# Channels grouped by five neighbours instead of by stride: input chunks turned before the first transform

## The chip, the cores and the metric

The kernel runs on one core of a Trainium2 chip. The core has five engines with queues of their own: TensorE (PE in the profile; its weight loads are listed apart as PEld), VectorE (DVE), ScalarE (ACT), GpSimd (POOL) and SyncE (SP, which only issues DMAs here). The metric is the device time of one execution in microseconds; three runs gave 457.33, 458.6 and 460.24, so the median is 458.6 us.

## The reference, cut to what matters

Eight sequences of 3200 positions with 256 channels go through a filter in the frequency domain and then through a gated linear unit whose gate is a short causal convolution:

```
X = rfft(x, axis=1);  Y = X * (filt_r + 1j*filt_i)
y = irfft(Y, n=3200, axis=1)
gate_pre[:, t] = sum over k of conv_w[k] * y[:, t-4+k]        # 5 taps, zeros in front
gate = 1 / (1 + exp(-gate_pre))
out  = (gate * (y @ w_val)) @ w_out
```

x and out are float32 of shape (8, 3200, 256), the filters (1601, 256), w_val and w_out (256, 256), conv_w (5, 256).

## The kernel before, in words

A sequence of 3200 is split as 128 x 25 (L = 128, R = 25): a transform of length 128, then one of length 25. The input of one batch lies in SBUF as a tile xb[128, 25, 260] in bf16: 25 rows of channels per partition, where 256 channels are padded to 260 = 52 x 5 (ND = 52, J = 5). The transform of length 25 is done for 5 channels at once, on 125 = 25 x 5 partitions (P2). Which five channels share a group is what the change is about: before, group g has the channels g, g + 52, g + 104, g + 156 and g + 208, so in the flattened free dimension of xb its 125 elements (25 rows, 5 channels) are one run with a step of 52. Eight chunks of 6 or 7 groups in turn (CH, line 24) cover the 52 groups of a batch.

One step G of the main loop (lines 470 to 492) handles one chunk in each stage of a software pipeline; a batch is eight steps, and there are 64 chunks:

- load_x (line 87): the rows of x for later batches, as GpSimd DMAs that cast float32 to bf16, two DMAs for nearly every row, 49 per batch. They are emitted some 25/8 rows per step, one batch ahead, into three buffers xb. The loads of batch 0 stand in the prologue.
- s1 (lines 315 to 325): for each group one matmul. The group's 125 strided elements are the stationary operand (lhsT), the cosine and sine table cf_t[128, 128] the moving one; the result is evicted by VectorE to sob.
- s2 (lines 327 to 354): four matmuls for the length 25, an eviction by ScalarE to xsb, and three products on VectorE (za, zb, z) with the filter tables fr_t and fm_t.
- inva (lines 356 to 373): the first half of the inverse, four matmuls per group in two column halves of 64, evicted by ScalarE to u[128, 25, 260].
- invb (lines 375 to 397): the second half, matmuls with a slice of u as stationary operand, evicted by ScalarE to yt; for the first piece of a batch, GpSimd copies four rows of yt for the convolution's history.
- conv (lines 399 to 414): the five taps as matmuls on 64 x 64 quarters of the array, sigmoid on ScalarE.
- val and outp (lines 416 to 452): the two dense layers, the gate product on VectorE between them, the output's eviction by VectorE (even pieces) or ScalarE (odd ones), and its DMA on SP.

The order within a step is written out by hand: load_x, invb, s1, conv, s2, val, inva, outp. A stage works on an older chunk the further back it stands: s2 one step behind s1, inva three, invb eleven (a batch must be complete), conv thirteen, val fourteen and outp fifteen. The framework gives each engine a queue in about this order and inserts the semaphores. All stages take their PSUM tile from one pool of four tiles (two banks each), in the order of the stages: a tile can be written once the eviction of the stage four tiles back is done.

Before the loop, a prologue makes the tables. For each of the two filters, GpSimd DMAs bring 13 + 12 rows in bf16 (lines 141 and 146), matmuls with a reversal matrix rev turn the order of 12 of them (line 233), an eviction puts them into gf (lines 239, 241), 52 matmuls with strided stationary operands turn the groups onto partitions (line 249), and further matmuls with a selection matrix ex (line 270) bring them into the order of the tables; ScalarE and VectorE evict.

Of the kernel before, what the change touches and what calls it, by code (L numbers as in the profile page):

```python
# [17 lines left out]
R = 25  # L18
J = 5
P2 = R * J  # L20
ND = 52
W = 66
UW = ND * J
# [8 lines left out]
def kernel(  # L32
# [47 lines left out]
    def load_x(b, r):  # L80
        xt = xb[b % NX]
        na = min(L, -(-(S - L * r) // R))
        for a0, a1, s in ((0, na, L * r), (na, L, L * r + R * na - S)):
            if a1 > a0:
                src = bass.AP(tensor=x.tensor, offset=x.offset + (b * S + s) * D,
                              ap=[[R * D, a1 - a0], [1, D]])
                nc.gpsimd.dma_start(out=xt[a0:a1, r, 0:D], in_=src)  # L87

    C2, S2, SN2 = (tb_t[0:P2, i].rearrange("p k j -> p (k j)") for i in (0, 1, 2))

    with tc.tile_pool(name="gen", bufs=1) as g1, tc.tile_pool(name="gen2", bufs=2) as g2:
# [45 lines left out]
        gf, gh = [], []  # L137
        for i, f in enumerate((filt_r, filt_i)):
            g = g1.tile([65, R, UW], BF16, name=f"gf{i}")
            nc.vector.memset(g[:, :, D:UW], 0.0)  # L140
# [4 lines left out]
            h = g1.tile([65, 12, D], BF16, name=f"gh{i}")  # L145
            nc.gpsimd.dma_start(
                out=h[...],
                in_=bass.AP(tensor=f.tensor, offset=f.offset + 64 * D,
                            ap=[[D, 65], [L * D, 12], [1, D]]))
            gh.append(h)  # L150
            gf.append(g)
        for t in xb:
            nc.vector.memset(t[:, :, D:UW], 0.0)
# [5 lines left out]
        for r in range(R):  # L159
            load_x(0, r)  # L160
# [55 lines left out]
        rev = g1.tile([128, 65], BF16, name="rev")  # L216
        nc.vector.tensor_scalar(rev[...], kt65[...], q64[:, 0:1], None, op0=ALU.is_equal)

        ps = psum()
# [5 lines left out]

        nc.vector.memset(fr_t[:, :, 65:W], 0.0)
        nc.vector.memset(fm_t[:, :, :, 65:W], 0.0)
        for i, g in enumerate(gf):
            gv = g[...].rearrange("p m d -> p (m d)")
            for h in range(3):  # L230
                ps = psum()
                for s in range(2):
                    nc.tensor.matmul(ps[0:65, 512 * s:512 * s + 512], lhsT=rev[0:65, :],
                                     rhs=gh[i][:, 4 * h + 2 * s:4 * h + 2 * s + 2, :],
                                     start=True, stop=True)
                dst = g[:, 13 + 4 * h:17 + 4 * h, 0:D]
                pv = ps[0:65, :].rearrange("p (m d) -> p m d", m=4)
                if i == 0:
                    nc.scalar.activation(dst, pv, AF.Copy)
                else:  # L240
                    nc.vector.tensor_copy(dst, pv)
            t1 = g1.tile([128, ND, 65], BF16, name=f"ft{i}")
            for h in range(4):
                ps = psum()
                for s, (o, n) in enumerate(((0, 6), (6, 7))):
                    for a in range(n):
                        d0 = 13 * h + o + a
                        lhs = gv[:, d0:d0 + (P2 - 1) * ND + 1:ND]
                        nc.tensor.matmul(ps[0:P2, 512 * s + 65 * a:512 * s + 65 * a + 65],
                                         lhsT=lhs, rhs=idb[0:65, 0:65],  # L250
                                         start=True, stop=True)
                for s, (o, n) in enumerate(((0, 6), (6, 7))):
                    dst = t1[0:P2, 13 * h + o:13 * h + o + n, :].rearrange(
                        "p g k -> p (g k)")
                    pv = ps[0:P2, 512 * s:512 * s + 65 * n]
                    if i == 0:
                        nc.scalar.activation(dst, pv, AF.Copy)
                    else:
                        nc.vector.tensor_scalar(dst, pv, sg[0:P2, 0:1], None, op0=ALU.mult)
            units = [(0, 3, 3), (3, 3, 3), (6, 3, 3), (9, 3, 3), (12, 3, 3),  # L260
                     (15, 4, 2), (19, 4, 2), (23, 2, 2)]
            for v in range(0, 8, 2):
                ps = psum()
                for s in range(2):
                    u0, nu, nt = units[v + s]
                    n = ND * nt
                    for uu in range(nu):
                        u = u0 + uu
                        w0 = (R - u) * J
                        nc.tensor.matmul(  # L270
                            ps[0:P2, 512 * s + n * uu:512 * s + n * (uu + 1)],
                            lhsT=exf[0:P2, w0:w0 + P2],
                            rhs=t1[0:P2, :, u:u + R * (nt - 1) + 1:R],
                            start=True, stop=True)
                    pv = ps[0:P2, 512 * s:512 * s + n * nu].rearrange(
                        "p (u g t) -> p g t u", u=nu, g=ND)
# [12 lines left out]
        cw = g1.tile([128, 2, K], FP32, name="cw")  # L289
        for dh in range(2):  # L290
# [1 line left out]
                out=cw[:, dh, :],  # L292
                in_=moe_conv_w[:, 128 * dh:128 * dh + 128].rearrange("k d -> d k"))
            for r in range(2):
                ch = 128 * dh + 64 * r
                nc.gpsimd.dma_start(  # L296
                    out=wv_t[:, dh, :].rearrange("p (r h j) -> p h r j", r=2, h=2)[:, r],
                    in_=moe_w_val[128 * dh:128 * dh + 128, 128 * r:128 * r + 128]
                    .rearrange("p (h j) -> p h j", h=2))
                nc.gpsimd.dma_start(out=wo_t[64 * dh:64 * dh + 64, r, :],  # L300
                                    in_=moe_w_out[ch:ch + 64, :])
# [10 lines left out]
    opool = ctx.enter_context(tc.tile_pool(name="ost", bufs=3))  # L312

    st = {}
    def s1(b, c):
        g0, nd = CH[c]
        xf = xb[b % NX][...].rearrange("p r d -> p (r d)")
        ps = psum()
        for i in range(nd):
            lhs = xf[:, g0 + i:g0 + i + (P2 - 1) * ND + 1:ND]  # L320
            nc.tensor.matmul(ps[0:P2, 128 * i:128 * i + 128], lhsT=lhs, rhs=cf_t[:, :],  # L321
                             start=True, stop=True)
        so = sob[(NF * b + c) % 4]
        nc.vector.tensor_copy(so[0:P2, 0:nd, 1:SW - 1],  # L324
# [30 lines left out]

    def inva(b, c):
        if c == 0:
            st[("U", b)] = upool.tile([128, R, UW], BF16, name="u")
        u = st[("U", b)]
        g0, nd = CH[c]  # L360
        z = st.pop(("Z", b, c))
# [1 line left out]
        for i in range(nd):  # L363
            o = 128 * i
            for lo, blk, s0, tab, first in ((0, 0, 1, C2, True), (64, 1, 0, C2, True),
# [1 line left out]
                nc.tensor.matmul(ps[lo:lo + 64, o:o + P2],  # L367
                                 lhsT=z[0:P2, blk, i, s0:s0 + 64], rhs=tab,
                                 start=first, stop=not first)
        nc.scalar.activation(  # L370
            u[:, :, :].rearrange("p r (j g) -> p r j g", j=J)[:, :, :, g0:g0 + nd],
            ps[:, :].rearrange("p (g m) -> p g m", m=128)[:, 0:nd, 0:P2]
            .rearrange("p g (r j) -> p r j g", j=J), AF.Copy)

    def invb(b, j):
        if j == 0:
# [77 lines left out]


    NS = NF * B
    for b in (0, 1):
        pass
    queue = [(b, r) for b in range(1, B) for r in range(R)]
    done = 0  # L460

# [6 lines left out]
    LAG_IA = 3  # L468
    LAG_IB = LAG_IA + NF
    for G in range(NS + LAG_IB + 8):  # L470
        want = min(len(queue), (G + 8) * R // NF)
        while done < want:
            load_x(*queue[done])
            done += 1
        c = back(G, LAG_IB)
        if c is not None:
            invb(*c)
        if G < NS:
            s1(*divmod(G, NF))
        c = back(G, LAG_IB + 2)  # L480
        if c is not None:
            conv(*c)
        if 0 <= G - 1 < NS:
            s2(*divmod(G - 1, NF))
        c = back(G, LAG_IB + 3)
        if c is not None:
            val(*c)
        if 0 <= G - LAG_IA < NS:
            inva(*divmod(G - LAG_IA, NF))
        c = back(G, LAG_IB + 4)  # L490
        if c is not None:
            outp(*c)


# [28 lines left out]
```

## Time and profile before

| | |
|---|---|
| median of three runs | 458.6 us (457.33 to 460.24) |
| the profiled execution | 458.49 us, of which the profile's span is 456.8 us |
| granted TensorE clock, mean | 0.998 |
| busy: PE / PEld / DVE / ACT / POOL | 421.6 / 316.5 / 296.0 / 255.4 / 222.5 us |
| S1 matmuls (line 321), 416 of them | 101.6 us busy, their weight loads 96.6 us |
| DMA issues of x on POOL (line 87), 392 of them | 201.8 us busy, 573 ns each |
| evictions: line 324 / 338 / 370 / 390 / 411 | 65.6 / 56.2 / 67.0 / 52.1 / 52.2 us |

How to read the lines that follow: a group line has the source line, the engine, the operation, output and input tiles, their shapes and the number of instructions; then busy time in us and the mean of one in ns; then the idle time of the engine just before these instructions, with what ended it. A timeline line has the start and the length in us, engine, line, operation and number of instructions merged into it. Listed lengths of matmuls and weight loads overlap each other, so the pace of a run of them is read from start to start. A line of the waits has the total in us, the number and the longest.

### The profile page before, as it was taken

The numbers are of one execution on the slowest core, as the hardware profiler recorded it, in microseconds if no ns is written. First come the engines' busy times: TensorE is split into PE (matmuls) and PEld (weight loads), VectorE is DVE, ScalarE is ACT, GpSimd is POOL, SyncE is SP. The second block draws the span as 40 slices with busy tenths as digits, with TensorE's granted clock in tenths as the row PEclk, the third lists the DMA queues.
The fourth block names the chain that finished last, engine by engine and source line by source line (L and its number), as shares of the span: only waits on it lengthen the run. The fifth ranks groups of instructions, "written<-read, shape, count | busy, mean of one in ns | idle before, by whom it ended". The sixth has DMA issues, their size and how long they took to land.

```text
span 456.8 us, 10880 instructions
## 1 busy us (share of the span) xinstructions
PE 421.6 (92%) x4616; PEld 316.5 (69%) x4647; DVE 296.0 (65%) x465; ACT 255.4 (56%) x287; POOL 222.5 (49%) x440
## 2 busy tenths in 40 slices
PE   0797879988999999999999999999999999999994
PEld 0585868876776767777777777777777776766562
DVE  8116368875766766676767677657776766766364
ACT  1320144566666666666566656566666566657852
POOL 7499999899997439901991089500010001000100
PEclk9999999999999999999999999999999999999999
DMA  8966656465587438711782158421212022113324
GB/s 100 88 64 60 67 63 69 52 68 59 63 159 139 93 68 156 143 70 56 132 157 70 72 99 156 101 82 47 93 66 86 7 89 82 71 47 127 145 115 193
DMA packets 49713, 41.99 MB, mean 92 GB/s; under 512 B 13390, under 2 KB 42496, under 8 KB 49664
## 3 DMA queue, kind: packets, MB, share of 16 engines
q0 software_dynamic: 40288, 15.07, 30.9%
q1 hardware_dynamic: 9376, 26.22, 14.5%
q8 instruction: 36, 0.59, 0.5%
q14 instruction: 13, 0.11, 0.1%
HBM read 30.07 MB, written 26.21 MB: 123 GB/s over the span
## 4 chain that ended last, share of the span: by engine, by line
PE 72%; POOL 20%; DMA 3%; ACT 2%; issue 1%; DVE 1%; DVEq 0%; POOLq 0%
POOL xb L87 18%; PE ps L321 16%; PE ps L406 13%; PE ps L367 10%; PE ps L440 9%; PE ps L423 9%; PE ps L388 5%; PE ps L333 4%; DMA gh<-in_filt_i_dram 3%; PE ps L335 2%; PE ps L334 2%; PE ps L336 2%; ACT u L370 2%; POOL wv_t L296 1%; POOL wo_t L300 0%
## 5 line engine op out<-in xcount | busy, mean ns | idle before, releaser
L87 POOL DMA_DIRECT2D xb<-in_x_dram x392 | 201.8, 573 | 59.6 <-PE ps L321 43.3
L428 DVE TENSOR_TENSOR gv<-ps,gt 128x1024 bf16<-128x1024 f32 (+1 forms) x56 | 62.2, 1111 | 72.9 <-PE ps L423 69.5
L321 PE MATMUL ps<-cf_t,xb 128*125 128x128 f16 x416 | 101.6, 385 | 0.0
L321 PEld LDWEIGHTS <-xb 128*125 128x125 bf16 x416 | 96.6, 312 | 1.2 <-issue 0.2
L411 ACT ACTIVATE gt<-ps 128x1024 bf16<-128x1024 f32 (+1 forms) x56 | 52.2, 933 | 70.5 <-PE ps L406 63.4
L324 DVE CAST sob<-ps 125x768 bf16<-125x768 f32 x64 | 65.6, 1025 | 31.8 <-PE ps L321 31.4
L370 ACT ACTIVATE u<-ps 128x750 bf16<-128x750 f32 x64 | 67.0, 1047 | 31.8 <-PE ps L367 31.7
L338 ACT ACTIVATE xsb<-ps 125x780 bf16<-125x780 f32 x64 | 56.2, 878 | 27.2 <-PE ps L336 24.2
L406 PE MATMUL ps<-yt,dg_t 64*64 64x512 bf16 (+1 forms) x1120 | 65.3, 358 | 1.4 <-POOL yt L397 1.4
L397 POOL COPY yt<-yt 128x508 bf16<-128x508 bf16 x16 | 9.7, 643 | 113.1 <-ACT yt L390 113.1
L367 PEld LDWEIGHTS <-z 125*64 125x64 bf16 x1664 | 48.7, 110 | 23.1 <-issue 22.4
L367 PE MATMUL ps<-tb_t,z 125*64 125x125 f16 x1664 | 59.1, 220 | 0.0
L390 ACT ACTIVATE yt<-ps 128x1024 bf16<-128x1024 f32 (+1 forms) x56 | 52.1, 930 | 12.1 <-PE ps L388 11.3
L440 PE MATMUL ps<-wo_t,gv 128*128 128x256 bf16 x400 | 53.3, 274 | 0.9 <-DVE gv L428 0.9
L423 PE MATMUL ps<-yt,wv_t 128*128 128x512 bf16 (+1 forms) x193 | 50.8, 352 | 1.7
L349 DVE TENSOR_TENSOR za<-xsb,fr_t 125x792 bf16<-125x792 bf16 x64 | 38.7, 604 | 15.0 <-ACT xsb L338 15.0
L440 PEld LDWEIGHTS <-gv 128*128 128x128 bf16 x400 | 35.2, 98 | 10.7 <-DVE gv L428 1.2
L406 PEld LDWEIGHTS <-dg_t 64*64 64x64 bf16 x1120 | 28.0, 106 | 18.9 <-issue 2.3
L352 DVE TENSOR_TENSOR z<-za,zb 125x792 bf16<-125x792 bf16 x64 | 39.1, 611 | 0.8
L445 DVE COPY o<-ps 128x1024 f32<-128x1024 f32 (+1 forms) x32 | 36.8, 1151 | 3.9 <-PE ps L440 3.9
L351 DVE TENSOR_TENSOR zb<-xsb,fm_t 125x792 bf16<-125x792 bf16 x64 | 38.8, 607 | 0.0
L388 PE MATMUL ps<-ci_t,u 128*128 128x128 f16 x400 | 31.8, 219 | 4.1 <-ACT u L370 4.1
(93 smaller groups left out, 341.2 us busy)
## 6 DMA issues: line engine op xcount, KB each, us to landing
out_dram<-o SPq DMA_DIRECT2D x32, 512.0 KB, 2.9
out_dram<-o SPq DMA_DIRECT2D x24, 384.0 KB, 2.3
xb<-in_x_dram POOLq DMA_DIRECT2D x8, 64.0 KB, 2.4
xb<-in_x_dram POOLq DMA_DIRECT2D x8, 61.5 KB, 2.6
xb<-in_x_dram POOLq DMA_DIRECT2D x8, 61.0 KB, 2.5
xb<-in_x_dram POOLq DMA_DIRECT2D x8, 59.0 KB, 2.4
xb<-in_x_dram POOLq DMA_DIRECT2D x8, 58.5 KB, 2.9
xb<-in_x_dram POOLq DMA_DIRECT2D x8, 56.5 KB, 2.5
```

The costliest lines, as they stand in the source:

```text
L87: nc.gpsimd.dma_start(out=xt[a0:a1, r, 0:D], in_=src)
L321: nc.tensor.matmul(ps[0:P2, 128 * i:128 * i + 128], lhsT=lhs, rhs=cf_t[:, :], start=True, stop=True)
L324: nc.vector.tensor_copy(so[0:P2, 0:nd, 1:SW - 1], ps[0:P2, 0:nd * 128].rearrange("p (g k) -> p g k", g=nd))
L338: nc.scalar.activation(xs[0:P2, :, 0:nd, 0:65], ps[0:P2, :].rearrange("p (c n) -> p c n", c=2)[:, :, 0:65 * nd] .rearrange("p c (g k) -> p ...
L367: nc.tensor.matmul(ps[lo:lo + 64, o:o + P2], lhsT=z[0:P2, blk, i, s0:s0 + 64], rhs=tab, start=first, stop=not first)
L370: nc.scalar.activation(u[:, :, :].rearrange("p r (j g) -> p r j g", j=J)[:, :, :, g0:g0 + nd], ps[:, :].rearrange("p (g m) -> p g m", m=12 ...
L388: nc.tensor.matmul(ps[:, o:o + L], lhsT=u[:, r, 128 * dh:128 * dh + 128], rhs=cw_[:, sh:sh + L], start=True, stop=True)
L406: nc.tensor.matmul(ps[64 * dh:64 * dh + 64, 512 * r:512 * r + np_ * L], lhsT=dg_t[rows, dh, k, :], rhs=y[rows, dh, p0 + k:p0 + k + np_, :] ...
L411: nc.scalar.activation(g[:, :, 0:np_ * L], ps[:, :].rearrange("p (h n) -> p h n", h=2)[:, :, 0:np_ * L], AF.Sigmoid)
L423: nc.tensor.matmul(ps[:, 512 * eh:512 * eh + np_ * L], lhsT=wv_t[:, dh, 128 * eh:128 * eh + 128], rhs=y[:, dh, H + p0:H + p0 + np_, :], st ...
L428: nc.vector.tensor_tensor(gv[:, :, 0:np_ * L], ps[:, :].rearrange("p (h n) -> p h n", h=2)[:, :, 0:np_ * L], g[:, :, 0:np_ * L], op=ALU.mult)
L440: nc.tensor.matmul(ps[:, D * a:D * a + D], lhsT=gv[:, eh, L * a:L * a + L], rhs=wo_t[:, eh, :], start=(eh == 0), stop=(eh == 1))
```

## The change

A group now holds five neighbouring channels: group g has the channels 5g to 5g + 4. The last group would reach over the end, so it takes the channels 251 to 255 (a helper, split, gives it apart), and the padding to 260 goes away. For S1's stationary operand, each chunk of x is first copied ("turned") from xb, where a group's five channels are a run in each of 25 rows, into a small tile xpb where the 125 elements of a group lie side by side. ScalarE does this for the even chunks and for all chunks of batch 0, GpSimd for the odd chunks of the other batches, two steps ahead of S1; there are four tiles xpb. The eviction of inva writes runs of whole groups; for the last chunk it is two instructions.

In the prologue, the filter rows come in float32 by SP DMAs instead of GpSimd DMAs with a cast; ScalarE (real part) and VectorE (imaginary part) turn them into the same grouped layout, each time in two instructions because of the last group; the reversal matmuls are in float32 now. The tile t1 has its two free dimensions exchanged, so that the next matmuls read runs of 52. The loads of x for batch 0 stand ahead of some memsets. The DMAs of w_val and w_out move from the prologue into step 0, behind the loads of batch 1.

In the loop, the order within a step becomes load_x, invb, s1, s2, val, outp, conv, inva, with the turn of the chunk two steps ahead in front: conv and inva, which use parts of the array, now follow each other.

```
-    xb = [cpool.tile([128, R, UW], BF16, name=f"xb{i}") for i in range(NX)]
+    xb = [cpool.tile([128, R, D], BF16, name=f"xb{i}") for i in range(NX)]
+    NP = 4
+    xpb = [cpool.tile([128, 7, P2], BF16, name=f"xpb{i}") for i in range(NP)]
...
+    def split(g0, nd):
+        if g0 + nd < ND:
+            return [(0, nd, J * g0)]
+        return [(0, nd - 1, J * g0), (nd - 1, nd, D - J)]
+
+    def permute(b, c):
+        g0, nd = CH[c]
+        xt = xb[b % NX]
+        xp = xpb[(NF * b + c) % NP]
+        for i0, i1, d0 in split(g0, nd):
+            dst = xp[:, i0:i1, :].rearrange("p g (r j) -> p g r j", j=J)
+            src = xt[:, :, d0:d0 + J * (i1 - i0)].rearrange("p r (g j) -> p g r j", j=J)
+            if c % 2 and b > 0:
+                nc.gpsimd.tensor_copy(dst, src)
+            else:
+                nc.scalar.activation(dst, src, AF.Copy)
...
-            g = g1.tile([65, R, UW], BF16, name=f"gf{i}")
-            nc.gpsimd.dma_start(
-                out=g[:, 0:13, 0:D],
+            g = g1.tile([65, 13, D], FP32, name=f"gd{i}")
+            nc.sync.dma_start(
+                out=g[...],
...
+            def turn(m0, nm, src):
+                for i0, i1, d0 in split(0, ND):
+                    ev(q[:, i0:i1, m0:m0 + nm, :],
+                       src[:, :, d0:d0 + J * (i1 - i0)].rearrange(
+                           "p m (g j) -> p g m j", j=J))
+            turn(0, 13, gd[i])
             for h in range(3):
                 ps = psum()
...
-                        lhs = gv[:, d0:d0 + (P2 - 1) * ND + 1:ND]
+                                         lhsT=qv[:, 13 * h + o + a, :],
...
 def s1(b, c):
-            lhs = xf[:, g0 + i:g0 + i + (P2 - 1) * ND + 1:ND]
-            nc.tensor.matmul(ps[0:P2, 128 * i:128 * i + 128], lhsT=lhs, rhs=cf_t[:, :],
+            nc.tensor.matmul(ps[0:P2, 128 * i:128 * i + 128], lhsT=xp[:, i, :], rhs=cf_t[:, :],
...
 def inva(b, c):
+        pv = ps[:, :].rearrange("p (g m) -> p g m", m=128)[:, :, 0:P2]
+        for i0, i1, d0 in split(g0, nd):
+            nc.scalar.activation(
+                u[:, :, d0:d0 + J * (i1 - i0)].rearrange("p r (g j) -> p r g j", j=J),
+                pv[:, i0:i1, :].rearrange("p g (r j) -> p r g j", j=J), AF.Copy)
...
     for G in range(NS + LAG_IB + 8):
+        if G == 0:
+            permute(0, 0)
+            permute(0, 1)
+        if G + 2 < NS:
+            permute(*divmod(G + 2, NF))
...
+        if G == 0:
+            load_w()
         c = back(G, LAG_IB)
         if c is not None:
             invb(*c)
         if G < NS:
             s1(*divmod(G, NF))
-        c = back(G, LAG_IB + 2)
-        if c is not None:
-            conv(*c)
         if 0 <= G - 1 < NS:
             s2(*divmod(G - 1, NF))
         c = back(G, LAG_IB + 3)
         if c is not None:
             val(*c)
-        if 0 <= G - LAG_IA < NS:
-            inva(*divmod(G - LAG_IA, NF))
         c = back(G, LAG_IB + 4)
         if c is not None:
             outp(*c)
+        c = back(G, LAG_IB + 2)
+        if c is not None:
+            conv(*c)
+        if 0 <= G - LAG_IA < NS:
+            inva(*divmod(G - LAG_IA, NF))
```

More of the change, by code (lines that the diff above doesn't have):

```diff
@@ L149 @@
                             ap=[[D, 65], [L * D, 12], [1, D]]))
+            gd.append(g)
             gh.append(h)
-            gf.append(g)
-        for t in xb:
-            nc.vector.memset(t[:, :, D:UW], 0.0)
+            gp.append(g1.tile([65, ND, R, J], BF16, name=f"gp{i}"))
+        for r in range(R):
+            load_x(0, r)
         for t in sob:
@@ L158 @@
             nc.vector.memset(t[:, :, :, 65:W], 0.0)
-        for r in range(R):
-            load_x(0, r)
         pr = g1.tile([128, 128], FP32, name="pr")
@@ L215 @@
         nc.vector.tensor_copy(idb[:, :], ident[:, :])
-        rev = g1.tile([128, 65], BF16, name="rev")
+        rev = g1.tile([128, 65], FP32, name="rev")
         nc.vector.tensor_scalar(rev[...], kt65[...], q64[:, 0:1], None, op0=ALU.is_equal)
@@ L227, with ev @@
         nc.vector.memset(fm_t[:, :, :, 65:W], 0.0)
-        for i, g in enumerate(gf):
-            gv = g[...].rearrange("p m d -> p (m d)")
+        for i in range(2):
+            def ev(dst, src, i=i):
+                if i == 0:
+                    nc.scalar.activation(dst, src, AF.Copy)
+                else:
+                    nc.vector.tensor_copy(dst, src)
+            q = gp[i]
+            def turn(m0, nm, src):
[4 more added lines that the diff above has]
+            turn(0, 13, gd[i])
             for h in range(3):
@@ L235 @@
                                      start=True, stop=True)
[L236 to L242, printed above, removed]
+                turn(13 + 4 * h, 4, ps[0:65, :].rearrange("p (m d) -> p m d", m=4))
+            qv = q[...].rearrange("p g m j -> p g (m j)")
+            t1 = g1.tile([128, 65, ND], BF16, name=f"ft{i}")
             for h in range(4):
@@ L246 @@
                     for a in range(n):
-                        d0 = 13 * h + o + a
-                        lhs = gv[:, d0:d0 + (P2 - 1) * ND + 1:ND]
                         nc.tensor.matmul(ps[0:P2, 512 * s + 65 * a:512 * s + 65 * a + 65],
-                                         lhsT=lhs, rhs=idb[0:65, 0:65],
-                                         start=True, stop=True)
+                                         lhsT=qv[:, 13 * h + o + a, :],
+                                         rhs=idb[0:65, 0:65], start=True, stop=True)
                 for s, (o, n) in enumerate(((0, 6), (6, 7))):
-                    dst = t1[0:P2, 13 * h + o:13 * h + o + n, :].rearrange(
-                        "p g k -> p (g k)")
-                    pv = ps[0:P2, 512 * s:512 * s + 65 * n]
+                    dst = t1[0:P2, :, 13 * h + o:13 * h + o + n]
+                    pv = ps[0:P2, 512 * s:512 * s + 65 * n].rearrange(
+                        "p (g k) -> p k g", g=n)
                     if i == 0:
@@ L272 @@
                             lhsT=exf[0:P2, w0:w0 + P2],
-                            rhs=t1[0:P2, :, u:u + R * (nt - 1) + 1:R],
+                            rhs=t1[0:P2, u:u + R * (nt - 1) + 1:R, :],
                             start=True, stop=True)
                     pv = ps[0:P2, 512 * s:512 * s + n * nu].rearrange(
-                        "p (u g t) -> p g t u", u=nu, g=ND)
+                        "p (u t g) -> p g t u", u=nu, g=ND)
                     def dst_ap(full):
@@ L314, with load_w @@
     st = {}
+    def load_w():
+        for dh in range(2):
+            for r in range(2):
+                ch = 128 * dh + 64 * r
+                nc.gpsimd.dma_start(
+                    out=wv_t[:, dh, :].rearrange("p (r h j) -> p h r j", r=2, h=2)[:, r],
+                    in_=moe_w_val[128 * dh:128 * dh + 128, 128 * r:128 * r + 128]
+                    .rearrange("p (h j) -> p h j", h=2))
+                nc.gpsimd.dma_start(out=wo_t[64 * dh:64 * dh + 64, r, :],
+                                    in_=moe_w_out[ch:ch + 64, :])
     def s1(b, c):
         g0, nd = CH[c]
-        xf = xb[b % NX][...].rearrange("p r d -> p (r d)")
+        xp = xpb[(NF * b + c) % NP]
         ps = psum()
         for i in range(nd):
-            lhs = xf[:, g0 + i:g0 + i + (P2 - 1) * ND + 1:ND]
-            nc.tensor.matmul(ps[0:P2, 128 * i:128 * i + 128], lhsT=lhs, rhs=cf_t[:, :],
+            nc.tensor.matmul(ps[0:P2, 128 * i:128 * i + 128], lhsT=xp[:, i, :], rhs=cf_t[:, :],
                              start=True, stop=True)
@@ L357, in inva @@
         if c == 0:
-            st[("U", b)] = upool.tile([128, R, UW], BF16, name="u")
+            st[("U", b)] = upool.tile([128, R, D], BF16, name="u")
         u = st[("U", b)]
@@ L456 @@
     NS = NF * B
-    for b in (0, 1):
-        pass
     queue = [(b, r) for b in range(1, B) for r in range(R)]
```

21 lines of the change are left out of this document (4 added, 17 removed).

## The prediction

> **What bounds the kernel now.** First the head of the page, and the stretch table for one period of eight steps (start, end, length, then busy time and instructions of PE, weight loads, DVE, ACT, POOL; granted clock, DMA share, GB/s).
>
> ```profile
> span 456.8 us, 10880 instructions
> PE 421.6 (92%) x4616; PEld 316.5 (69%) x4647; DVE 296.0 (65%) x465; ACT 255.4 (56%) x287; POOL 222.5 (49%) x440
> ...
> 286.00:333.90 47.90, 47.26 (x557) 35.19 (x562) 32.88 (x44) 29.97 (x33) 5.63 (x12) 1.00 0.24 77
> ```
>
> One batch is eight steps. Their first S1 matmuls start at 142.36, 190.24, 238.12 and 285.99 us in the chain of waits, so a batch takes 47.9 us, and TensorE is busy for 47.26 of them at full granted clock. DVE and ACT have 15 to 18 us to spare. TensorE's own sequence sets the pace. Second, the groups with shapes kept apart, for what the sequence is made of.
>
> ```profile
> L321 PEld LDWEIGHTS <-xb 128*125 128x125 bf16 x416 | 96.6, 312 | 1.2 <-issue 0.2
> L249 PEld LDWEIGHTS <-gf 65*125 65x125 bf16 x104 | 23.0, 314 | 5.7 <-DVE gf L241 3.6 <-ACT gf L239 2.1
> L334 PEld LDWEIGHTS <-tb_t 125*125 125x125 f16 x64 | 9.0, 141 | 0.0
> L367 PEld LDWEIGHTS <-z 125*64 125x64 bf16 x1664 | 48.7, 110 | 23.1 <-issue 22.4 <-DVE zb L351 0.3 <-DVE z L352 0.3
> ```
>
> A weight load of 125 columns lists 312 ns where the columns lie 52 elements apart (L321, L249) and 141 ns where they lie side by side (L334). Third, the timeline of a steady step, for paces.
>
> ```profile
> 260.41 0.51 PE L388 MATMUL ps<-ci_t,u 128*128 128x128 f16 x6
> 260.51 1.14 ACT L370 ACTIVATE u<-ps 128x875 bf16<-128x875 f32 x1 [0.80 <-PE ps L367]
> 260.70 1.61 PEld L321 LDWEIGHTS <-xb 128*125 128x125 bf16 x7
> ...
> 260.76 1.70 PE L321 MATMUL ps<-cf_t,xb 128*125 128x128 f16 x7
> ...
> 262.38 1.27 PE L406 MATMUL ps<-yt,dg_t 64*64 64x512 bf16 x20
> ```
>
> Seven S1 matmuls take 260.76 to 262.38, 0.231 us each. L388 streams the same 128 columns at 0.058 (six in 0.35). L249 streams only 65 columns and still needs 0.2215 (52 in 11.52), so the load sets S1's pace, not the matmul. Fourth, POOL's timeline, since the chain gives POOL 18%, all before 108 us.
>
> ```profile
> 6.12 2.72 POOL L87 DMA_DIRECT2D xb<-in_x_dram  x5
> ...
> 18.55 21.66 POOL L87 DMA_DIRECT2D xb<-in_x_dram  x42 [1.41 <-DMA gh<-in_filt_i_dram]
> ...
> 45.05 34.68 POOL L87 DMA_DIRECT2D xb<-in_x_dram  x67
> ...
> 106.52 1.60 POOL L397 COPY yt<-yt 128x508 bf16<-128x508 bf16 x2
> ```
>
> The input's DMAs leave POOL at 0.516 us each (42 in 21.66), stand behind the filter DMAs until 18.55, and the first convolution waits for the two copies at 106.52, behind 164 of them.
>
> **The change, steady part, per batch.** *S1.* Its 52 groups take 12.0 us now (four chunks of six at 1.36 to 1.41, four of seven at 1.62). No row has a 125-column load side by side beside a matmul of 128. Bounds: 0.058 (L388) and 0.141 (L334's listed time, nothing overlapped). Listed times stand above paces: L321 312 against 231, L367 110 against 33 (28 loads from 283.19 to 284.11). Taking 78 off 141 gives 0.063; I take 0.062, so 3.2 us: **-8.8** (-9.0 to -4.7). The Trainium skill, TensorE: Matmul & The Clock Gate, § LDWEIGHTS (loading the stationary operand), has a load take columns / 1.2 ns, an estimate of 104 ns here and 5.4 us a batch, 2.2 less gain. L367's 64-column loads come faster than that rule's 53 ns, but in two column halves in turn, so the trace does not decide.
>
> *Mode changes.* Convolution with four rows lasts 262.38 to 263.59, 1.21 us, with three 0.94; the difference 0.27 is one row, four are 1.08, and 0.13 remains for entering and leaving. Conv and inva become neighbours, one change in four goes: 0.1 a step, **-0.8** (0 to -1.0).
>
> *invb behind inva.* The first invb of a batch needs the last inva's eviction. Now outp (0.66 to 0.88) lies between and TensorE still waits 0.5 a batch ("PE ps L388 <- ACT u L370: 4.1, 8"). That cover goes: the eviction (1.09, plus a second instruction of about 0.3 for the last group) starts when inva ends and nothing follows: 1.5. **+1.0** (+0.5 to +1.8). Queued behind it on TensorE is the whole step.
>
> *Turning and evictions.* Four even chunks of 750 elements on ACT: 0.80 (L448, 768 elements) to 1.01 (L370, 750), so 3.6. L370 writes longer runs now; its minimum is 804 ns, its median 1075; I give it -1. ACT goes from 30.0 to 32.6. The odd chunks go to POOL: L397 copies 508 elements in 606 to 643 ns, so 875 about 1.05, POOL 25.3 + 1.3 + 4.4 = 31. DVE's two-input operations suffer beside a POOL copy:
>
> ```profile
> 106.35 1.30 DVE L352 TENSOR_TENSOR z<-za,zb 125x924 bf16<-125x924 bf16 x1
> ```
>
> Its mean is 0.66. The Trainium skill, SBUF — State Buffer, § Who interferes with whom, says that a DVE instruction with two SBUF inputs contends with a GpSimd instruction that reads SBUF; this row agrees. By the Trainium skill a product could be held for a turn's whole 1.05, an estimated 1.6 a batch more. By the row, four times 0.65 brings DVE to 35.5. All stay below TensorE's 39, but PSUM has four tiles: outp waits for invb's eviction. In a step with a turn, ACT has sigmoid 0.93, inva 0.81, turn 0.85, invb 0.93 after conv ended; by then TensorE, with invb 0.42, S1 0.38, s2 0.84 and val 0.96 behind inva 0.8, comes to outp some 0.35 us too early. DVE's steps (sob, gv, o and three products, 5.1 of 5.5 us) add the like in the other parity. I take 0.7 a pair of steps: **+2.8** (0, if ACT turns in its idle time, to +6, below).
>
> Sum: -8.8 - 0.8 + 1.0 + 2.8 = -5.8 a batch. From step 15 to 63 it is 6.1 batches: **-35.4**.
>
> **Start.** POOL's x loads begin at about 2.2 instead of being held to 18.55. In its order: 49 loads to 27.5, 49 to 52.8, eight weight loads (5.0, as 40.06 to 45.05) to 57.8, 36 loads to 76.4, the first turn on POOL to 77.5. So S1 of step 9 can't start before 77.5 (89.5 now), and step 15, behind two more turns, the two copies and 48 loads, not before 101 (117.3 now). Until then ACT turns all chunks: 0.88 + 1.0 + 0.9 = 2.8 a step against 3.17 now. The filter part: 2 x 52 strided loads fall from 11.5 to 3.3 us, but the evictions behind them (eight of 0.52 on ACT, 0.65 on DVE) hold 4.2 and 5.2: -13.6. The turns of 13 rows (3315 elements, 3.1 us by L390's 1.02 for 1024) lie beside the filters' landing and idle DVE time; those from PSUM add 1 to 2. The six rev matmuls per filter become fp32, which no row shows: between nothing and the stage's whole gain of 7; I take 3 each. The filters come by SP; I leave their landings at 13 and 18. Net -6: first S1 at 57 instead of 63.4, step 9 at 82, and by step 15 **-10** (-4 to -13). Moved at no cost: conv_w's DMAs stand behind four filter DMAs on SP now, the two weights behind 49 x loads on POOL; their readers are the first conv and val, near 97 us, and 58 us is early enough. The removed memsets (0.1 each) lay in DVE's idle time. The tail without S1 keeps its work: **-1** for modes.
>
> The profiled execution took 458.49 us (span 456.8), the median of three is 458.6, so no shift: 458.5 - 35.4 - 10 - 1 = **412 us**.
>
> **Rivals.** *A: loads stay the bound.* With 0.141 S1 is 7.3, the evictions then stall less (+1.5): -4.7 - 0.8 + 1.0 + 1.5 = -3.0, times 6.1 = -18.3, in all **429**. For it: L334 lists 141 every time; against: it is hidden at a pace of 0.17, and listed times run above paces. By the 104 ns of the Trainium skill (the page named under S1) it would be an estimated 418. *B: evictions bind.* The turns and their neighbours wait in ACT's and DVE's queues for +6 a batch: -2.6, -15.9 in all, **432**. For it: ACT 32.6 and DVE 35.5 of 42 with four PSUM tiles; against: a queue has two steps of slack for the turns. *C: slower.* A turn reads runs of five; if POOL takes a time per run instead of per element, it holds DVE's products each time: DVE's 32.9 + 4P passes 47.9 at P = 3.8 us, that is 21 ns for each of 175 runs. At P = 6 DVE needs 56 minus overlaps of some 4: +4 a batch, +25 - 10 - 1, **472**. For it only that no row has such runs; against: 1.2 ns an element at L397, and L370 on ACT copies runs of six without such a price. That contiguous columns don't load faster at all is excluded by L334.
>
> **Chances.** Forecast 0.56 (alone 394 to 424), A 0.17, B 0.17, C 0.07, and 0.03 for something between B and C that is no change. Low end: S1 -9.0, modes -1.0, invb +0.5, evictions +1: -8.5, -51.9, start -13: 392, which I cut to 394; the high end takes in A and B: 437. A measurement tells about 1% from no change. Faster 0.90, same 0.03, slower 0.07.
>
> **What would show it.** S1 matmuls 0.06 apart; a batch of 42 us; conv and inva back to back; invb waiting 1.5 for L370's successor once a batch; POOL's first turn near 77 us, after two batches of loads; the turns near 0.9 on ACT and 1.05 on POOL, with za, zb or z up to twice as long beside them. It would be wrong with S1 at 0.1 or more, TensorE waiting for PSUM evictions each step, or POOL turns of several us.

## The result, and the profile after

The changed kernel takes 416.88 us (median of four runs, 415.85 to 417.31) against 459.01 us (four runs, 457.33 to 460.24): a ratio of 0.908, 95% interval 0.905 to 0.912. The forecast was 412, the range 394 to 437. The profiled execution took 416.61 us, its span is 414.9.

The total hides two errors that nearly cancel. By S1's first matmul of a step in the two timelines:

| | before | after | difference | predicted |
|---|---|---|---|---|
| step 15 starts | 117.13 | 119.63 | +2.5 | -10 |
| steps 15 to 63 (six batches) | 287.25 | 243.18 | -44.1 | -35.4 |
| from step 63 to the end of the span | 52.4 | 52.1 | -0.3 | -1 |

The -35.4 is 6.1 times 5.8, so it counts step 63 as well; for the six batches of that row the forecast's own figure is -34.8.

First, the head of the page of the changed kernel, with the granted clock in 40 slices.

```profile
span 414.9 us, 11040 instructions
PE 357.3 (86%) x4628; PEld 241.1 (58%) x4659; DVE 304.7 (73%) x465; ACT 274.4 (66%) x338; POOL 249.2 (60%) x471
...
PEclk9999999979699999999999999999999999999998
```

And the stretch table of the changed kernel: one late batch, and two stretches of the start (start, end, length, then busy time of PE, weight loads, DVE, ACT, POOL; granted clock, DMA share, GB/s).

```profile
303.15:343.22 40.07, 38.24 (x556) 26.55 (x560) 32.78 (x44) 31.04 (x39) 5.40 (x8) 1.00 0.21 84
...
90.00:95.00 5.00, 5.00 (x45) 3.76 (x45) 2.68 (x4) 2.12 (x3) 5.00 (x10) 0.58 0.52 53
...
110.00:115.00 5.00, 5.00 (x58) 3.12 (x57) 0.00 (x0) 1.98 (x3) 5.00 (x11) 0.53 0.39 39
```

A late batch takes 40.07 us instead of 47.9, TensorE is still the busiest with 38.24 of them, ACT has 31.0 and DVE 32.8. In the start the clock falls to nearly half in the two stretches shown, where the row of the kernel before is full. (Ahead of about 70 us both rows show it full only because the trace lists the clock from there on; the paces of that stretch are those of half the clock, see the last section.)

Second, the groups of the changed kernel with shapes kept apart, which answer to those of before.

```profile
L348 PEld LDWEIGHTS <-xpb 128*125 128x125 bf16 x416 | 32.0, 145 | 17.8 <-POOL xpb L103 9.4 <-issue 7.0 <-ACT xpb L105 0.2
L272 PEld LDWEIGHTS <-gp 65*125 65x125 bf16 x104 | 11.2, 229 | 5.8 <-DVE gp L249 3.0 <-ACT gp L247 2.8
L361 PEld LDWEIGHTS <-tb_t 125*125 125x125 f16 x64 | 9.1, 142 | 2.4 <-issue 2.4
L399 ACT ACTIVATE u<-ps 128x750 bf16<-128x750 f32 x40 | 32.1, 803 | 1.6 <-PE ps L394 0.7 <-issue 0.3
L105 ACT ACTIVATE xpb<-xb 128x750 bf16<-128x750 bf16 x33 | 27.6, 840 | 10.3 <-DMA xb<-in_x_dram 7.9 <-PE ps L348 2.5
L103 POOL COPY xpb<-xb 128x875 bf16<-128x875 bf16 x21 | 21.8, 1039 | 41.2 <-PE ps L348 41.2
```

S1's load lists 145 ns instead of 312, as L361 does. The turns cost 0.84 us on ACT and 1.04 on POOL.

Third, the timeline of two steady steps of the changed kernel.

```profile
242.62 0.57 PE L348 MATMUL ps<-cf_t,xpb 128*125 128x128 f16 x7
243.03 0.34 PE L360 MATMUL ps<-sob,tb_t 125*125 125x390 bf16 x1
...
245.54 1.27 PE L434 MATMUL ps<-yt,dg_t 64*64 64x512 bf16 x20
246.74 0.87 PE L394 MATMUL ps<-tb_t,z 125*64 125x125 f16 x24
247.55 0.51 PE L416 MATMUL ps<-ci_t,u 128*128 128x128 f16 x6
248.67 0.51 PE L348 MATMUL ps<-cf_t,xpb 128*125 128x128 f16 x6 [0.61 <-DVE o L473]
...
252.62 1.42 POOL L103 COPY xpb<-xb 128x875 bf16<-128x875 bf16 x1
...
253.30 1.25 DVE L379 TENSOR_TENSOR z<-za,zb 125x924 bf16<-125x924 bf16 x1
```

Seven S1 matmuls take 242.62 to 243.03, 0.0586 us each. conv (L434) and inva (L394) stand back to back. At 248.67 S1 waits 0.61 us for outp's eviction, because its PSUM tile isn't free; this wait is new. z beside a POOL turn takes 1.25 us instead of its mean of 0.70.

Fourth, POOL's timeline in the start of the changed kernel, and TensorE's waits (total in us, number, longest).

```profile
3.05 3.61 POOL L88 DMA_DIRECT2D xb<-in_x_dram  x7
11.76 0.53 POOL L88 DMA_DIRECT2D xb<-in_x_dram  x1 [5.10 <-DMA xb<-in_x_dram]
...
26.03 38.04 POOL L88 DMA_DIRECT2D xb<-in_x_dram  x74 [0.74 <-DMA xb<-in_x_dram]
...
88.97 0.93 POOL L103 COPY xpb<-xb 128x875 bf16<-128x875 bf16 x1
...
108.28 1.90 POOL L425 COPY yt<-yt 128x508 bf16<-128x508 bf16 x2
```

```profile
PE ps L348 <- POOL xpb L103: 8.9, 3, 6.7
PE ps L416 <- ACT u L399: 7.1, 8, 0.9
PE ps L348 <- DVE o L473: 5.2, 6, 1.1
PE ps L434 <- POOL yt L425: 2.8, 1, 2.8
```

POOL's loads are held by landings in the first 26 us, its first turn comes at 88.97 instead of 77.5, and the yt copies at 108.28, where they were before (106.52). The first and the last line of the waits are the start: 11.7 us.

### The profile page after: what moved, and what is told of

The parts are those of the page before. It is cut to its first block, busy times and chain, and to the rows that moved or that the text cites. A ratio compares the mean times of both kernels' runs of the same rounds, so it can differ in the third digit from the quotient of the medians.

```text
span 414.9 us, 11040 instructions
## 1 busy us (share of the span) xinstructions
PE 357.3 (86%) x4628; PEld 241.1 (58%) x4659; DVE 304.7 (73%) x465; ACT 274.4 (66%) x338; POOL 249.2 (60%) x471
## 4 chain that ended last, share of the span: by engine, by line
PE 52%; POOL 21%; DVE 13%; DMA 6%; issue 4%; ACT 3%; DVEq 0%; ACTq 0%; POOLq 0%
POOL xb L88 18%; PE ps L434 10%; PE ps L451 8%; PE ps L394 8%; PE ps L468 7%; DMA xb<-in_x_dram 6%; PE ps L416 5%; DVE o L473 4%; PE ps L348 4%; DVE za L376 2%; PE ps L360 2%; DVE zb L378 2%; PE ps L363 2%; PE ps L362 2%; PE ps L361 2%
## 5 line engine op out<-in xcount | busy, mean ns | idle before, releaser
L88 POOL DMA_DIRECT2D xb<-in_x_dram x392 | 203.9, 551 | 18.0 <-DMA xb<-in_x_dram 11.7
L103 POOL COPY xpb<-xb 128x875 bf16<-128x875 bf16 (+2 forms) x35 | 30.3, 869 | 72.1 <-PE ps L348 72.1
L434 PE MATMUL ps<-yt,dg_t 64*64 64x512 bf16 (+1 forms) x1120 | 66.6, 362 | 3.0 <-POOL yt L425 2.8
L394 PEld LDWEIGHTS <-z 125*64 125x64 bf16 x1664 | 49.9, 112 | 26.6 <-issue 25.7
L394 PE MATMUL ps<-tb_t,z 125*64 125x125 f16 x1664 | 60.7, 223 | 0.4 <-PE ps L363 0.4
L399 ACT ACTIVATE u<-ps 128x750 bf16<-128x750 f32 (+2 forms) x72 | 57.1, 793 | 2.8 <-PE ps L394 0.7
L348 PE MATMUL ps<-cf_t,xpb 128*125 128x128 f16 x416 | 37.2, 231 | 14.9 <-POOL xpb L103 8.9
L468 PEld LDWEIGHTS <-gv 128*128 128x128 bf16 x400 | 38.9, 98 | 14.3 <-DVE gv L456 1.5
L376 DVE TENSOR_TENSOR za<-xsb,fr_t 125x792 bf16<-125x792 bf16 x64 | 40.4, 631 | 5.4 <-ACT xsb L365 4.7
L434 PEld LDWEIGHTS <-dg_t 64*64 64x64 bf16 x1120 | 28.4, 107 | 27.0 <-issue 14.5
L379 DVE TENSOR_TENSOR z<-za,zb 125x792 bf16<-125x792 bf16 x64 | 43.3, 676 | 1.1
L348 PEld LDWEIGHTS <-xpb 128*125 128x125 bf16 x416 | 32.0, 145 | 17.8 <-POOL xpb L103 9.4
L378 DVE TENSOR_TENSOR zb<-xsb,fm_t 125x792 bf16<-125x792 bf16 x64 | 40.5, 632 | 0.0
## 6 DMA issues: line engine op xcount, KB each, us to landing
xb<-in_x_dram POOLq DMA_DIRECT2D x8, 61.5 KB, 2.6
```

The costliest lines, as they stand in the source:

```text
L88: nc.gpsimd.dma_start(out=xt[a0:a1, r, :], in_=src)
L348: nc.tensor.matmul(ps[0:P2, 128 * i:128 * i + 128], lhsT=xp[:, i, :], rhs=cf_t[:, :], start=True, stop=True)
L394: nc.tensor.matmul(ps[lo:lo + 64, o:o + P2], lhsT=z[0:P2, blk, i, s0:s0 + 64], rhs=tab, start=first, stop=not first)
L399: nc.scalar.activation(u[:, :, d0:d0 + J * (i1 - i0)].rearrange("p r (g j) -> p r g j", j=J), pv[:, i0:i1, :].rearrange("p g (r j) -> p r ...
L434: nc.tensor.matmul(ps[64 * dh:64 * dh + 64, 512 * r:512 * r + np_ * L], lhsT=dg_t[rows, dh, k, :], rhs=y[rows, dh, p0 + k:p0 + k + np_, :] ...
L468: nc.tensor.matmul(ps[:, D * a:D * a + D], lhsT=gv[:, eh, L * a:L * a + L], rhs=wo_t[:, eh, :], start=(eh == 0), stop=(eh == 1))
```

## The experiments

The theory after the result: **in the late batches only S1's weight loads changed the time, and in the start GpSimd's queue binds**, because its turns and copies stand behind DMAs of x. The rivals: the order of the calls carries part of the gain; evictions are already the next bound; the start is limited by the prologue on TensorE. In what follows a batch is the mean distance of equal steps in the last three batches (47.88 us before, 40.06 after), and step 15 is where its S1 starts.

### The order of the calls

```
 s1
+conv            # as before
 s2, val
+inva
 outp
-conv, inva
```

> The changed kernel with the order of calls in a step as before (conv right behind S1, inva behind val and ahead of outp); regrouping and turning stay. Theory (the steady gain is the weight loads of S1 alone): a batch goes from 40.1 us to about 40.5, +0.8 for one mode change a step, -0.4 for the cover that invb gets back; 417 to 420 us. Rival (the order carries a real part of the 7.8 us a batch, through waits on evictions): 42 us a batch or more, 428 us or more.

Measured: 415.66 us (ratio to before 0.904, 0.902 to 0.907), a batch of 39.68. The rival fell by far; the sign of the theory's small term was wrong too: the old order is faster by 0.38 us a batch.

### S1 side by side in the kernel before

```
-lhs = xf[:, g0+i : g0+i + (P2-1)*ND + 1 : ND]
+lhs = xf[:, P2*(g0+i) : P2*(g0+i) + P2]
```

> The kernel before with one edit: the 125 columns of each S1 load are read side by side instead of 52 elements apart. It leaves out the regrouping, so S1 transforms other elements than the reference wants; there is no turning and all else stays. Theory: S1 takes 3.05 us a batch instead of 12.0, a batch 39.0 us, nothing comes in its place, the start stays (step 15 at 117): 459 - 6.1 x 8.9 = 405 us, 402 to 409. Rival (with S1 short, the evictions of other steps bind even without turns): 42 us a batch, 423 us.

Measured: 415.10 us (0.904, 0.901 to 0.907). The time missed the theory by 10 us, while its batch is 39.50, near the 39.0 expected. TensorE's waits in this kernel:

```profile
PE ps L406 <- POOL yt L397: 17.6, 2, 11.8
...
PE ps L388 <- ACT u L370: 4.1, 8, 1.2
```

Two convolutions wait 17.6 us for POOL's yt copies. These come at 105.98 and 152.40, within 0.7 us of their places before (106.52 and 151.76). So the wall stood in the kernel before as well, where TensorE came late enough to wait only 1.4 us for yt. A faster S1 runs into it.

The two runs split the late batch: S1's loads -8.38 (before to here), turning and the grouped evictions together +0.18 (here to the first run, both in the old order), the new order +0.38 (the first run to the change). The 0.38 belongs to the new order and GpSimd's turns together: without these turns a batch takes 39.68 us in both orders (the next run, and the old order without GpSimd below).

### Turns on ScalarE alone

```
-if c % 2 and b > 0: nc.gpsimd.tensor_copy(dst, src)
-else:               nc.scalar.activation(dst, src, AF.Copy)
+nc.scalar.activation(dst, src, AF.Copy)
```

> The changed kernel with all turns on ScalarE, none on GpSimd. Theory: the waits of steps 9, 11 and 13 for GpSimd's turns (8.9 us) go, but the first conv still waits for GpSimd's two yt copies, which come only some 3 us earlier (105 instead of 108); ScalarE goes from 31 to about 34.5 us of 40 a batch, 0 to +0.5 a batch. 412 to 416 us. Rival (evictions bind): ScalarE's 3.5 us more a batch are paid in full, 21 us, 430 us or more.

Measured: 412.63 us (0.897, 0.894 to 0.901), a batch of 39.68, and the first conv waits 8.2 us for yt. ScalarE has 3.1 us more a batch (34.1 of 39.7 us) and it costs nothing: the sum of ScalarE's work doesn't bind. Two early batches (steps 23 to 39), 41.06 and 41.04 us in the change, take 39.68 and 39.69 here, where the late ones differ by 0.38: a turn that POOL does among its DMAs of x costs more, about 1 us a batch.

### The loads four steps later

```
-want = min(len(queue), (G + 8) * R // NF)
+want = min(len(queue), (G + 4) * R // NF)
```

> The changed kernel with the input loads issued four steps later in the loop (12 row groups, 24 DMAs, some 12.4 us less ahead of each turn and copy on GpSimd). Theory (the start is lost in GpSimd's program order): GpSimd's first turn at 76.6 us instead of 89.0, the yt copies at 96 instead of 108, TensorE's waits of 8.9 + 2.8 us near steps 9 to 14 go, steady batches stay at 40.1: 405 to 411 us. Rival (the prologue and the pace of steps 0 to 14 bind anyway): 415 to 417 us.

Measured: 418.25 us (0.911, 0.908 to 0.914): the time missed, no gain. Yet the start went as expected. POOL's timeline in this kernel:

```profile
75.32 0.94 POOL L103 COPY xpb<-xb 128x875 bf16<-128x875 bf16 x1
...
96.30 1.52 POOL L425 COPY yt<-yt 128x508 bf16<-128x508 bf16 x2
...
193.74 1.16 POOL L425 COPY yt<-yt 128x508 bf16<-128x508 bf16 x2
```

The first turn comes at 75.3, the yt copies at 96.3, and step 15 at 107.4 instead of 119.6. But one batch (steps 23 to 31) then takes 55.7 us: the yt copies of the third batch come at 193.74 (189.93 in the change), and the conv there waits 8.9 us. In POOL's queue 139 loads instead of 164 stand before the copies of the first batch, but 294 before those of the third in both kernels. Less work ahead of the first turn was more ahead of a later one, and POOL, busy almost without a gap until about 200 us, sets the step. The theory had to be widened from the queue's order at the start to its whole load.

### GpSimd with loads only

The turns go to ScalarE as above, and:

```
-nc.gpsimd.memset(y[:, :, 0:H, 0:1], 0.0)
+nc.vector.memset(y[:, :, 0:H, 0:1], 0.0)
-    nc.gpsimd.tensor_copy(y[:, dh, 0:H, 1:L], ...)
+    nc.vector.tensor_copy(y[:, dh, 0:H, 1:L], ...)
```

> The changed kernel with the turns on ScalarE and the two yt copies (and their memset) on VectorE, so that GpSimd issues only the input's DMAs and the weights'. Theory (up to step 30 GpSimd's queue binds: 8 x 49 loads at 0.52 us, with the turns and the yt copies among them): the waits for yt (8.2 + 1.8 us with the turns alone moved) go, step 15 comes at 108 instead of 115.8, batches stay at 39.7: 400 to 404 us. Rival (the landing of the loads themselves, or the filling of the stages, binds): the wait moves to the turns' loads or to other evictions, 408 to 413 us.

Measured: 397.19 us (0.866, 0.863 to 0.869), 4.7% under the change, a little better than expected; step 15 at 104.7, a batch of 39.68. No wait for POOL is left; the page's clock row and the longest steady waits in this kernel:

```profile
PEclk9999999999999999999999999999999999999999
```

```profile
PE ps L413 <- ACT u L396: 8.0, 8, 1.7
PE ps L357 <- DVE o L470: 1.7, 7, 0.6
```

That settles the start: step 15 comes 12.4 us earlier than before, where 10 were predicted, as soon as POOL has nothing to do that TensorE waits for.

### The bf16 reversal

```
-gh (float32, from the DMA) and rev in float32
+nc.vector.tensor_copy(gh[i], ghf[i])     # to bf16
+rev in bf16
```

> The changed kernel with the filter's second half cast to bf16 by VectorE and turned with a bf16 rev matrix. Theory (GpSimd's queue binds after step 8): the first S1 comes 8 to 12 us earlier, near 51 (both filters' rev matmuls 2.8 us instead of 10.5), but GpSimd's turns and the yt copies stay where they are (89 and 108 us) and TensorE waits for them: 414 to 417 us. Rival (the prologue on TensorE binds): the gain stays, 405 to 409 us.

Measured: 417.35 us (0.910, 0.908 to 0.913): as the theory has it, just above its 414 to 417. The first S1 starts at 51.0 instead of 61.5, then S1 waits 16.3 us for POOL's first turn, at 90.45. The prologue is not what bound.

### A filter that hardly loads

```
 g: out=g[:, 0:1, :] of 13 rows, the others zeroed by VectorE
 h: out=h[:, 0:1, :] of 12 rows, the others zeroed by VectorE
```

> The changed kernel with 1 of 13 and 1 of 12 filter row groups loaded per filter and zeros in the others: it leaves out most of the filter, so the products are other numbers; every matmul, turn and eviction stays. Theory (the filter's DMAs on SyncE's queue slow the input's landings, and GpSimd waits for these): the first 49 loads leave GpSimd by 28 us instead of 38, its first turn comes near 79 instead of 89, the yt copies near 98 instead of 108. Rival (the loads hold each other up without the filter): the first turn within 2 us of 89.

Measured in one execution: 411.19 us. POOL's timeline in this kernel:

```profile
2.85 51.19 POOL L88 DMA_DIRECT2D xb<-in_x_dram  x97
...
78.85 1.97 POOL L103 COPY xpb<-xb 128x875 bf16<-128x875 bf16 x1 [0.59 <-PE ps L350]
...
98.92 1.90 POOL L427 COPY yt<-yt 128x508 bf16<-128x508 bf16 x2
```

The loads run through without a hold, the first turn comes at 78.85, 10.1 us earlier. So SyncE's four float32 filter DMAs slowed the landings of x, for which POOL waited; what the two kinds of DMA share was not tried. The added memsets put the first S1 off to 66.4, so the time itself tells less.

### The price by stride

```
+sd = (1, 2, 4, 8, 16, 26, 32, 52)[c]
 lhs = xf[:, g0+i : g0+i + (P2-1)*sd + 1 : sd]
```

> The kernel before with the 125 columns of an S1 load 1, 2, 4, 8, 16, 26, 32 and 52 elements apart in chunks 0 to 7 of every batch: it leaves out the grouping, so S1 transforms other elements; all else stays. In the late batches, pace of one S1 matmul. Theory (the price belongs to the bytes from one column to the next, up to some limit): 0.059 at 1, rising by steps, 0.23 at 52, and the same from 32 bytes on (16 elements and more). Rival (any stride but 1 costs the same, a switch): 0.23 at 2 and at all others.

Measured in one execution: 444.49 us. The timeline, one chunk a line, with strides of 52, 1, 2, 4, 8, 16, 26 and 32 elements:

```profile
253.93 1.70 PE L322 MATMUL ps<-cf_t,xb 128*125 128x128 f16 x7
260.47 0.51 PE L322 MATMUL ps<-cf_t,xb 128*125 128x128 f16 x6
265.78 0.58 PE L322 MATMUL ps<-cf_t,xb 128*125 128x128 f16 x7
270.39 0.81 PE L322 MATMUL ps<-cf_t,xb 128*125 128x128 f16 x6
276.28 1.76 PE L322 MATMUL ps<-cf_t,xb 128*125 128x128 f16 x7
282.57 1.56 PE L322 MATMUL ps<-cf_t,xb 128*125 128x128 f16 x6
287.75 1.91 PE L322 MATMUL ps<-cf_t,xb 128*125 128x128 f16 x7
293.74 1.44 PE L322 MATMUL ps<-cf_t,xb 128*125 128x128 f16 x6
```

From the chunk's start to the start of the next line on TensorE (mostly conv, so a mode change is in it), divided by the matmuls: 0.073 us at 1, 0.074 at 2, 0.123 at 4, 0.243 at 8, 0.233 at 16, 0.261 at 26, 0.228 at 32; the loads list 137, 138, 208, 322, 326, 347 and 304 ns, and 312 at 52. The switch fell: a stride of 2 is free and 4 costs half. The theory is right that the price rises by steps and then stays (0.228 to 0.261), but the step is complete at 8 elements (16 bytes), not at 16. The Trainium skill, SBUF — State Buffer, § Door 1: The DMA port swizzle, has lines of 16 bytes, which need two hits each for full bandwidth, and so calls strides up to 8 bf16 elements free. The runs agree on the 16 bytes as the end of the rise; a stride of 8 elements, with one hit a line, pays the whole price here, and 4, with two hits, pays half.

### The order again, without GpSimd

The kernel in which GpSimd issues only loads, with the order of the first experiment.

> The kernel in which GpSimd issues only loads, with the order of calls as before (conv right behind S1, inva ahead of outp). Theory (the order is worth nothing by itself: a mode change of some 0.1 us a step against the waits of invb and S1, 1.3 us a batch here): a batch stays between 39.4 and 39.9 us, 396 to 399 us. Rival (the waits are the larger part): 38.9 us a batch or less, 391 to 393 us.

Measured: 396.73 us (0.864, 0.862 to 0.865), a batch of 39.68 in both orders. The stretch 264.16 to 303.84 of the kernel in the new order, then of this one:

```profile
264.16:303.84 39.68, 38.45 (x564) 26.57 (x562) 33.20 (x47) 34.08 (x44) 0.00 (x0) 1.00 0.21 84
```

```profile
264.16:303.84 39.68, 39.55 (x564) 26.93 (x562) 32.66 (x47) 34.26 (x44) 0.00 (x0) 1.00 0.21 84
```

TensorE is busy 1.1 us less in the new order and waits 1.1 us more. Fewer mode changes are a real gain on TensorE (0.14 us a step by this), and the waits that the same order brings take all of it. Why the two cancel so exactly was not followed.

### Two tries to go on

The bf16 reversal on the kernel in which GpSimd issues only loads:

> The kernel in which GpSimd issues only loads, with the bf16 rev matrix and the filter's second half cast by VectorE. Theory (with GpSimd's queue free of turns and copies, the prologue on TensorE sets the start, and the float32 rev matmuls cost about 8 us): first S1 near 51, step 15 near 95 instead of 104.7, batches 39.7: 386 to 390 us. Rival (the loads of the second batch, which leave GpSimd by about 62 us, or the pace of the first steps take it back): 393 to 398 us.

Measured: 395.97 us (0.860, 0.855 to 0.864); the four executions are 391.31, 395.80, 396.14 and 396.22, and the profiled one is the first. In it the first S1 starts at 50.7 and step 15 at 96.5. There 6.0 us of the 8 last to the end; in the other three, 1.0 to 1.4. These have no trace; their mean granted clock is 0.987 or 0.988 instead of 0.999. The twin below shows where such a gain can go, but that theirs went there is not shown.

S1 and s2 ahead of invb, on the same kernel:

```
-invb, s1, s2, val
+s1, s2, invb, val
```

> The kernel in which GpSimd issues only loads, with S1 and s2 ahead of invb in a step. Theory (invb waits 0.9 us a batch for the eviction of the last inva; S1 and s2, 1.2 us, lie ahead of it then): the wait goes, a batch takes 38.7 to 39.0 us, 390 to 393 us. Rival (another eviction is late by as much, S1 for a PSUM tile first of all): 39.6 us a batch, 396 to 398 us.

Measured: 398.16 us (0.867, 0.865 to 0.868), a batch of 40.13 to 40.20. The wait for u goes from 8.0 to 1.3 us, and s2 waits more for outp's eviction, as its PSUM tile has one stage less of lead:

```profile
PE ps L357 <- DVE o L470: 4.9, 11, 0.7
PE ps L448 <- DVE sob L348: 1.6, 6, 0.3
```

TensorE is idle 1.28 us a batch, nearly as before (1.23), and busy 0.4 us longer. The timelines show where: S1's chunks, behind inva now, last 0.45 and 0.40 us without a wait, instead of 0.40 and 0.34 behind invb, eight times a batch. So S1 pays for standing behind inva; by what mechanism was not tried. The rival's mechanism holds, the result is a little worse than it said.

Both edits together:

> Both edits on the kernel in which GpSimd issues only loads: the bf16 rev matrix, and S1 and s2 ahead of invb. Theory (the two gains lie in different places, the prologue and the late batches): they add up, 380 to 384 us, first S1 near 51, batches of 38.8. Rival (one of them falls as above): 386 to 393 us.

Measured: 396.18 us (0.862, 0.860 to 0.864); nothing adds up. The first S1 starts at 51.0, step 15 at 96.0, and then one batch takes 46.1 us. ACT's timeline there:

```profile
102.09 1.68 ACT L102 ACTIVATE xpb<-xb 128x750 bf16<-128x750 bf16 x2 [5.04 <-DMA xb<-in_x_dram]
```

ACT's turn of the third batch waits 5 us for the landing of its loads: three batches, 147 loads at 0.52 us, have left POOL only at 99.5. So POOL's queue, with nothing but loads in it, binds again once the start comes some 8 us earlier. Near 396 us is what these edits reach.

## Why the prediction was right, and where it was wrong

**S1, -8.8 a batch: right.** The pace is 0.0586 against 0.062 taken; S1 itself fell from 12.0 to 3.0 us (four chunks at 0.41, four at 0.34). The batch gained 8.38 when this was changed alone. The rest is the order: with conv behind S1, conv starts only 0.50 or 0.44 us after S1's chunk does, so S1 takes 3.7 us a batch there, and the difference to 12.0 is nearly all of the 8.38. The slow loads had hidden this step to conv. *Rival A* fell with it: contiguous loads don't bind at 0.141 beside the matmul of 128 columns. The 104 ns by the Trainium skill, weighed there, don't hold for this stream at full clock; they are near the 0.106 us at half the clock (last section).

**Mode changes, -0.8, and invb, +1.0: right as a sum, and for nearly the reasons given.** Measured -1.1 and +1.1 without GpSimd's turns, +0.38 with them. The wait of invb is 0.9 instead of 1.5; the other part is one that was not named, S1 behind outp's eviction.

**Turning and evictions, +2.8: this term was mis-sized.** It is +0.18 in the old order; in the new one GpSimd's turns bring the 0.38 besides. The durations were right (ACT 0.84 against 0.9, POOL's turns 1.04 against 1.05, z up to twice as long), and the step from a longer queue on ACT and DVE to a wait of TensorE was wrong: both have idle time in each step, and ACT took 3.1 us a batch more for nothing. *Rival B*, the same at +6, fell. *Rival C*, a price per run of five on POOL, fell with the turns at 1.04 us. Together the four terms measured -7.8 in the late batches and -7.35 over all six, since POOL's turns cost more while it issues loads.

**The start, -10: this step failed.** It came out at +2.5. Three of its premises were wrong. The loads of x were to leave POOL by 27.5 unhindered; the filter's DMAs on SyncE slowed them and cost 10 us (shown by loading less of it). The fp32 reversal was taken at +3 us a filter; 10.48 us stand against 2.72 in bf16 for the first, +7.8, just over the upper bound given. The Trainium skill, FP8 and Floating Point Precision, § TensorE Precision Notes, states four passes for true FP32; the trace agrees with a ratio of 3.9. And the 52 loads of a filter took 5.8 us instead of 11.7, 0.111 each, where 3.3 for the loads and 4.2 and 5.2 for the evictions were taken: the 0.062 is a pace of the full clock, and the prologue doesn't have it (last section). But only the first mattered: with bf16 the prologue was 10.5 us shorter and the time the same. That POOL's queue sets steps 8 to 15 was named in the prediction with its sum; what failed is that its start was taken as free.

**The total** came within 1.2% of the forecast by luck: the start lost 12.5 us against it, and the six batches gained 8.7 on it.

## What to carry to other kernels

Before a stage is made faster, look at which other queue will be late next and add up all that stands in it: GpSimd's 392 DMA issues take 204 us, and with copies among them that TensorE waits for, 20 of the 62 us that the runs reached were lost until every copy left that queue. A term for a longer queue on an engine with idle time in each step was near zero here; take it so until a run shows otherwise. The new order and S1 first were both worth nothing: what each gained came back as waits in other places. For a bf16 stationary operand, the step from column to column matters up to 16 bytes: keep it at 4 bytes or less.

## What the runs showed of the hardware

- After waits in the start the granted clock fell: 0.58 in the stretch 90 to 95 us, behind a wait of 6.66 us, and 0.53 in 110 to 115, behind one of 2.76; matmuls there took twice their time (seven S1 in 0.81 us instead of 0.41). So an early wait costs more than its length. The length alone doesn't decide: with the bf16 reversal and GpSimd free of copies, TensorE waited 2.8 us ahead of 100.5 us, and the clock stayed at 1.00 from 95 to 105. The Trainium skill, TensorE: Matmul & The Clock Gate, § What's actually happening, has half the clock after an idle window of some 3.4 us; the second case is shorter by the wait alone, though in the 5.7 us ahead of 109.33 TensorE had only 1.3 us of work.
- 52 contiguous loads of 125 columns in the prologue (L272, with matmuls of 65 columns between) come 0.111 us apart, in the late S1 0.0586. The difference is the clock, for early S1 chunks of the changed kernel have the slow pace too:

```profile
67.75 0.95 PE L348 MATMUL ps<-cf_t,xpb 128*125 128x128 f16 x7
68.49 0.53 PE L360 MATMUL ps<-sob,tb_t 125*125 125x390 bf16 x1
```

Seven matmuls in 0.74 us are 0.106 each. That is close to the 0.81 for seven right behind the first long wait, where the granted clock was 0.50 (87.39 to 94.22). The matmuls of s2 with 390 columns come 0.33 us apart at 69 us as well, and 0.17 at 74 us. So TensorE ran at half the clock up to about 70 us, though no clock is listed there. The strided loads before don't follow the clock: 0.2215 us in the prologue (L249), 0.231 in the late batches.
